# A ReLU² attention with a gated convolution FFN: products that read the two halves of their moving tile in turn

## The chip, the cores and the metric

The kernel runs on one core of a Trainium2 chip. The metric is device time in microseconds (us). PE is TensorE (products), DVE is VectorE, ACT is ScalarE, POOL is GpSimd, SP is SyncE, which issues most of the DMAs here.

## What is computed

Two stages on a batch of 4 sequences with 3136 positions, all in fp32. The first is an attention with squared ReLU in place of softmax, gated by `u`; the second a feed-forward layer whose gate is a convolution over three neighbouring positions.

```python
def _attn_ref(u, v, z):          # u, v: 4 x 3136 x 256; z: 4 x 3136 x 64
    scale = 1.0 / S
    scores = scale * np.matmul(z, z.transpose(0, 2, 1))
    attn = np.maximum(scores, 0.0) ** 2
    out = np.matmul(attn, v)
    return (u * out).astype(np.float32)

def _moe_ref(x, w_in, conv_w, w_out):   # 256 -> 1024 -> 256
    h = np.maximum(x @ w_in, 0.0)
    ...
    for k in range(K):
        conv_out += conv_w[k][None, None, :] * hp[:, k:k + S, :]
    gate = 1.0 / (1.0 + np.exp(-conv_out))
    return (h * gate @ w_out).astype(np.float32)
```

## The kernel before

Positions lie along the free axis. A batch has 6 blocks of 512 positions (`NB`) and a rest of 64; a block meets 25 tiles of 128 keys (`NJ`), so there are 24 x 25 = 600 slots. A slot takes one tile of keys through the attention for one block, and the feed-forward work of the block before is dealt out over the same slots.

To keep fp32 accuracy with `float32r` products, each operand is split into a high part and a low part (what the high part left over), and a product is made of two or three: high times high, low times high, high times low. Per slot:

- `scores`: two products of 512 columns (`zh`, then `zl`, against the block's queries `zq`) into PSUM. Since the scores are symmetric, many tiles are not computed but fetched: what was computed earlier is cut into halfwords by POOL (`part`), written to DRAM by SP (`spill`) and read back transposed (`fetch`). Such a tile stands in `tp`.
- `relu` and `square`: ACT brings the scores to SBUF with a ReLU (`t<-s`), DVE multiplies scores and ReLU in place in PSUM (`s<-s,t`). For a fetched tile, ACT or DVE squares `tp` into PSUM.
- `split_hi`, `split_lo`: ACT copies the square to `ah` (the high part), DVE subtracts it for `al` (the low part).
- `attend`: for each half of the 256 value columns, three products against `vv` accumulate in `av0`, `av1` over the block's 25 slots.

Per block and each of 8 groups `f` of 128 features: `ffn_in` (six products), `ffn_relu` (ACT from PSUM to SBUF), the three taps of the convolution and the gate (ACT, DVE), `ffn_hi` and `ffn_lo` (ACT, POOL), `ffn_out` (three products for each output half), and at the block's end `evac` and a store. The last 64 positions of all batches are done apart: `rem_scores`, `rem_attend` (25 products a batch whose moving tile is `vv`), and a feed-forward of 256 and 266 columns at the very end. `early` and `ring_score` make small pieces of a block's scores ahead of time. Seven products on zeros (`warm`) open the program.

Every product has its own weight load of 128 x 128. A moving tile is read in natural order, column after column, 512 columns of 4 bytes, or 256 or 266 in the small cases; `ring_score` reads two runs of 128. The product's columns come out in the same order, and ACT and DVE read PSUM contiguously.

The order on each engine is written out by hand: `ev` holds the calls of each slot in six classes, `LA`, `LT`, `LS` and the like say how many slots ahead each step stands, and the loop over `k` at the end issues them. Nothing is rescheduled afterwards. Every engine works through its instructions in that order; PSUM has two banks for scores (`s`), two for `ph`, and two each for `av` and `o`.

Of the kernel before, what the change touches and what calls it, by code (L numbers as in the profile page):

```python
# [81 lines left out]
def kernel(  # L82
# [94 lines left out]


    zst, vst, wst, wps = {}, {}, {}, {}
    LO, HI = slice(0, DQ), slice(DQ, P)  # L180
# [54 lines left out]
    def warm():  # L235
        x = mv.tile([P, NB], F32R, tag="gh", name="wx", bufs=3)
        nc.vector.memset(x.bitcast(F32), 0.0)
        o = ps.tile([P, 512], F32, tag="o0", name="wo")
        for _ in range(WARM):
            nc.tensor.matmul(o, lhsT=x[:, :P], rhs=x, start=True, stop=True)  # L240

# [108 lines left out]
    def ring_score(blk):  # L350
        j = blk % QB * CB + CB - 1
        dg[blk] = p = ps.tile([P, 512], F32, tag="ph", name="ph", bufs=2)
        w = slice(j * P, (j + 1) * P)
        nc.tensor.matmul(odd(p), lhsT=zh[:, w], rhs=odd(zq[blk]), start=True, stop=False)
        nc.tensor.matmul(odd(p), lhsT=zl[:, w], rhs=odd(zq[blk]), start=False, stop=True)

    def ring_relu(blk):
        p = dg[blk]
        dg[blk] = t = wk.tile([P, 1, 2 * NB], U16, tag="dg", name="dg", bufs=1)
        nc.scalar.activation(odd(t[:, 0].bitcast(F32)), odd(p), AF.Relu, scale=SC1)  # L360

# [12 lines left out]
    def scores(k):  # L374
# [9 lines left out]
        w, c = slice(j * P, (j + 1) * P), own_cols(k)  # L384
        r = zq[blk][:, c]
        nc.tensor.matmul(s[:, c], lhsT=zh[:, w], rhs=r, start=True, stop=False)  # L386
        nc.tensor.matmul(s[:, c], lhsT=zl[:, w], rhs=r, start=False, stop=True)  # L387
        sc[k] = s

    rl, pl, dq, dd, tp = {}, {}, {}, {}, {}  # L390

# [12 lines left out]
    def part(k):  # L404
# [45 lines left out]
    def relu(k):  # L450
        x = side(k)
        if at_slot(k)[2] or x or held(k):
            if held(k):
                rl[k] = tp[k] = hs.pop(at_slot(k)[0])
            if x and x < CB - 1:
                rl[k] = tp[k]
                c = own_cols(k)
                nc.scalar.activation(tp[k][:, c], sc[k][:, c], AF.Relu, scale=SC1)
            else:
# [5 lines left out]
            else:  # L465
                nc.scalar.activation(sc[k][:, :NB], tp[k], AF.Square, scale=SC1**-0.5)
            return
        rl[k] = wk.tile([P, NB], F32, tag="t", name="t", bufs=3)
        nc.scalar.activation(rl[k], sc[k][:, :NB], AF.Relu, scale=SC1)  # L469
# [15 lines left out]
    def split_hi(k):  # L485
# [17 lines left out]
    def attend(k, dcs=None):  # L503
# [5 lines left out]
        for dc in dcs or (reversed(range(DC)) if first or k == NJ - 1 else range(DC)):  # L509
# [13 lines left out]
    def early(blk):  # L523
        hs[blk] = p = ps.tile([P, 512], F32, tag="ph", name="ph", bufs=2)
        nc.tensor.matmul(p, lhsT=zp, rhs=zq[blk], start=True, stop=True)  # L525

    def early_copy(blk):
        p = hs[blk]
        hs[blk] = c = wk.tile([P, NB], F32, tag="st", name="sc", bufs=4)
        nc.scalar.copy(c, p)  # L530

# [72 lines left out]
    def rem_evac():  # L604
        rr.pop("a")
        rr["t"] = t = wk.tile([P, NB], F32, tag="t", name="re", bufs=3)
        nc.scalar.copy(t, rr.pop("o"))

# [33 lines left out]
    def gate_x(blk, eng):  # L642
        gate_half(blk, 0)
        t, o = ut[blk], pav.pop(blk)
        x = wk.tile([P, NB], F32, tag="t", name="x1", bufs=3)
        nc.scalar.mul(x, o[1], SCALE)
# [31 lines left out]
    def ffn_in(blk, f, tag="ph"):  # L678
# [3 lines left out]
        for dc in range(DC):  # L682
            nc.tensor.matmul(o, lhsT=wih[:, dc, w], rhs=xh[blk][:, dc], start=(dc == 0), stop=False)  # L683
            nc.tensor.matmul(o, lhsT=wil[:, dc, w], rhs=xh[blk][:, dc], start=False, stop=False)  # L684
        for dc in range(DC):
            nc.tensor.matmul(o, lhsT=wih[:, dc, w], rhs=xl[blk][:, dc], start=False, stop=(dc == DC - 1))  # L686
        ph[blk, f] = p
# [17 lines left out]
    def ffn_relu(blk, f):  # L705
        t, p = hb[blk, f], ph[blk, f]
        if blk == "r":
            nc.scalar.activation(seam(t)[:, :, 2 : 2 + RQ], seam(p[:, : B * RQ]), AF.Relu)
            return
        nc.scalar.activation(t[:, 2 : NB + 2], p, AF.Relu)  # L710

# [39 lines left out]
    def ffn_out(blk, f, dc, tag="o"):  # L751
# [3 lines left out]
        h, l = gg[blk, f]  # L755
        nc.tensor.matmul(o, lhsT=wol[:, f, d], rhs=h, start=(f == 0), stop=False)  # L756
        nc.tensor.matmul(o, lhsT=woh[:, f, d], rhs=h, start=False, stop=False)  # L757
        nc.tensor.matmul(o, lhsT=woh[:, f, d], rhs=l, start=False, stop=(f == FC - 1))  # L758
        if dc == DC - 1:
# [10 lines left out]
    def evac(blk, dcs=range(DC), engs=(nc.scalar, nc.scalar)):  # L770
# [7 lines left out]
        for dc in dcs:  # L778
            copy(engs[dc], ob[blk][:, dc, :e], po[blk][dc][:, :e])

# [356 lines left out]
```

## Time and profile before

| | |
|---|---|
| median of 3 runs | 1530.1 us (1529.99 to 1530.73) |
| span of the profiled execution | 1528.4 us |
| PE busy | 1518.8 us, 99%, 6781 products |
| ACT busy | 1210.8 us, 79% |
| DVE busy | 1114.9 us, 73% |
| POOL busy | 859.7 us, 56% |
| DMA queue of SP | 56.0% of 16 engines' span |

The span runs from the first to the last instruction of one profiled execution; the times are of whole runs without a profile, 1.7 us above it in the median. Engines work at once, so shares don't add up. A product is shown on PE with its full length, 0.39 us for 512 columns, but the next one starts before it ends: what a product costs in a row of products is the distance between starts. PEld is the weight load, which runs beside the products. In rows of instructions, `av<-ah,vv` gives the tile written and the tiles read, and `128x512` partitions and elements.

### The profile page before, as it was taken

Reading aid. Unit: us, or ns where it says so; the run is one execution under the profiler, and the core shown is the slowest. Engines: PE = TensorE matmul, PEld = TensorE weight load, DVE = VectorE, ACT = ScalarE, POOL = GpSimd, SP = SyncE. Lnnn points to the kernel's source line nnn. Section 1 sums busy time; section 2 is a strip of 40 time slices with the busy share of each in tenths; the row PEclk is TensorE's granted clock in tenths of the full one; section 3 lists DMA queues with packets and bytes.
Section 4 is the critical chain, followed back from the end, with each engine's and each line's share of the span. In section 5 each row is a group of like instructions: output and inputs, shape, how many; then the busy total and the mean of one; then the engine's idle time right before and its main releaser. Section 6 shows DMA issues by size and latency. Waiting matters only on the chain.

```text
span 1528.4 us, 22846 instructions
## 1 busy us (share of the span) xinstructions
PE 1518.8 (99%) x6781; PEld 1255.5 (82%) x6781; DVE 1114.9 (73%) x1714; ACT 1210.8 (79%) x2308; POOL 859.7 (56%) x1174
## 2 busy tenths in 40 slices
PE   9999999999999999999999999999999999999998
PEld 7778888888888888888888888888888888888887
DVE  8987767777777666767777766776777676677767
ACT  8888787788777878877878777877787777877767
POOL 7775555557755554555866554555586654545434
PEclk9999999999999999999999999999999999999999
DMA  6543576774545467678344565666644546466631
GB/s 201 163 141 96 150 156 144 154 164 126 157 119 140 125 138 159 141 146 183 116 143 120 143 149 125 151 154 132 155 148 134 128 122 150 120 150 151 128 67 35
DMA packets 435902, 211.03 MB, mean 138 GB/s; under 512 B 331456, under 2 KB 412608, under 8 KB 435776
## 3 DMA queue, kind: packets, MB, share of 16 engines
q1 hardware_dynamic: 435104, 209.17, 56.0%
q8 instruction: 53, 0.87, 0.2%
q14 instruction: 73, 0.60, 0.1%
q10 hardware_dynamic: 672, 0.40, 0.1%
HBM read 36.59 MB, written 86.90 MB: 81 GB/s over the span
## 4 chain that ended last, share of the span: by engine, by line
PE 96%; ACT 2%; DVE 1%; issue 1%; DMA 0%; POOL 0%; SPq 0%; ACTq 0%; POOLq 0%
PE av L514 51%; PE o L756 6%; PE o L757 6%; PE o L758 6%; PE ph L683 6%; PE ph L684 6%; PE ph L686 6%; PE s L386 4%; PE s L387 4%; PE av L596 1%; ACT t L469 0%; DVE ph L725 0%; PE ph L525 0%; DMA st<-in_z_dram 0%; ACT ah L492 0%
## 5 line engine op out<-in xcount | busy, mean ns | idle before, releaser
L514 PE MATMUL av<-ah,vv 128*128 128x512 f32 x2400 | 735.0, 390 | 1.9 <-ACT ah L492 1.6
L173 DVE TENSOR_TENSOR al<-s,ah 128x512 fp32r<-128x512 f32 x576 | 396.9, 689 | 312.0 <-PE av L514 165.8
L514 PEld LDWEIGHTS av<-ah,vv 128*128 128x128 f32 x2400 | 446.9, 188 | 93.4 <-ACT ah L492 2.0
L514 PE MATMUL av<-al,vv 128*128 128x512 f32 x1152 | 448.4, 389 | 0.1
L173 POOL TENSOR_TENSOR gl<-hb,gh 128x512 fp32r<-128x512 f32 x192 | 253.1, 1318 | 158.7 <-ACT gh L176 158.4
L725 DVE SCALAR_TENSOR_TENSOR ph<-hb,cw,ph 128x512 f32<-128x512 f32 x384 | 286.8, 747 | 5.0 <-ACT ph L720 4.4
L416 POOL COPY pl<-t 128x1024 uint16<-128x1024 uint16 (+1 forms) x257 | 261.9, 1021 | 1.8 <-DMA dq<-pl 1.6
L514 PEld LDWEIGHTS av<-al,vv 128*128 128x128 f32 x1152 | 216.3, 188 | 45.8 <-DVE al L173 0.6
L483 DVE TENSOR_TENSOR s<-s,t 128x512 f32<-128x512 f32 x275 | 191.9, 698 | 71.7 <-ACT t L469 69.9
L469 ACT ACTIVATE t<-s 128x512 f32<-128x512 f32 x277 | 165.9, 599 | 75.1 <-PE s L387 66.8
L492 ACT CAST ah<-s 128x512 fp32r<-128x512 f32 x277 | 163.5, 590 | 57.6 <-DVE s L483 57.2
L715 POOL COPY halo<-hb 128x2 f32<-128x2 f32 x160 | 31.1, 195 | 279.6 <-ACT hb L710 279.4
L732 ACT ACTIVATE ph<-ph 128x512 f32<-128x512 f32 (+1 forms) x200 | 115.6, 578 | 87.3 <-DVE ph L725 84.1
L488 ACT ACTIVATE ah<-tp 128x512 fp32r<-128x512 f32 x278 | 174.1, 629 | 3.0 <-PE av L514 2.7
L683 PE MATMUL ph<-xh,wih 128*128 128x512 f32 x384 | 149.9, 390 | 0.6 <-DVE hb L739 0.6
L756 PE MATMUL o<-gh,wol 128*128 128x512 f32 x384 | 149.8, 390 | 0.0
L684 PE MATMUL ph<-xh,wil 128*128 128x512 f32 x384 | 149.8, 390 | 0.0
L757 PE MATMUL o<-gh,woh 128*128 128x512 f32 x384 | 149.4, 389 | 0.0
L758 PE MATMUL o<-gl,woh 128*128 128x512 f32 x384 | 149.4, 389 | 0.0
L710 ACT ACTIVATE hb<-ph 128x512 f32<-128x512 f32 x192 | 114.6, 597 | 29.1 <-PE ph L686 27.6
L739 DVE TENSOR_TENSOR hb<-ph,hb 128x512 f32<-128x512 f32 x192 | 131.7, 686 | 5.5 <-ACT ph L732 0.7
L720 ACT ACTIVATE ph<-hb,cw 128x512 f32<-128x512 f32 x192 | 133.5, 695 | 0.3
(138 smaller groups left out, 2084.3 us busy)
## 6 DMA issues: line engine op xcount, KB each, us to landing
dq<-pl SPq DMA_DIRECT2D x232, 256.0 KB, 2.7
st<-in_v_dram SPq DMA_DIRECT2D x48, 256.0 KB, 3.1
ut<-in_u_dram SPq DMA_DIRECT2D x24, 512.0 KB, 4.0
out_dram<-ob SPq DMA_DIRECT2D x19, 512.0 KB, 3.8
st<-in_z_dram SPq DMA_DIRECT2D x24, 256.0 KB, 3.2
sh<-sc SPq DMA_DIRECT2D x44, 128.0 KB, 2.4
dd<-pl SPq DMA_DIRECT2D x69, 64.0 KB, 2.0
dd<-pl SPq DMA_DIRECT2D x23, 192.0 KB, 2.5
```

Of the source, the lines that this page charges most:

```text
L173: eng.tensor_tensor(out=out, in0=a, in1=b.bitcast(F32), op=ALU.subtract)
L416: nc.gpsimd.tensor_copy(pl[k], src.bitcast(U16).rearrange("p (n h) -> p h n", h=2))
L469: nc.scalar.activation(rl[k], sc[k][:, :NB], AF.Relu, scale=SC1)
L483: nc.vector.tensor_tensor(out=s, in0=s, in1=rl[k], op=ALU.mult)
L488: nc.scalar.activation(ah[k], tp.pop(k), AF.Square, scale=SC1**-0.5)
L514: nc.tensor.matmul(o, lhsT=w[:, j, d], rhs=r, start=first and i == 0, stop=last and i == len(ops) - 1)
L683: nc.tensor.matmul(o, lhsT=wih[:, dc, w], rhs=xh[blk][:, dc], start=(dc == 0), stop=False)
L684: nc.tensor.matmul(o, lhsT=wil[:, dc, w], rhs=xh[blk][:, dc], start=False, stop=False)
L725: nc.vector.scalar_tensor_tensor(out=c, in0=hb[blk, f][:, k : e + k], scalar=cw[:, f, k : k + 1], in1=c, op0=ALU.mult, op1=ALU.add,)
L756: nc.tensor.matmul(o, lhsT=wol[:, f, d], rhs=h, start=(f == 0), stop=False)
L757: nc.tensor.matmul(o, lhsT=woh[:, f, d], rhs=h, start=False, stop=False)
L758: nc.tensor.matmul(o, lhsT=woh[:, f, d], rhs=l, start=False, stop=(f == FC - 1))
```

## The change

Every moving tile is now read through `pairs`: column 0, then the first column of the second half, column 1, the second of the second half, and so on. For 512 columns the two are 1 KB apart in a partition; for 256 columns 512 bytes, for 266 columns 532. In `rem_attend` the halves are the high and low part of `vv`. The 64-column products are left as they are. Weights, accumulation, the number of products and their order stay.

The columns in PSUM then stand as 0, 256, 1, 257. They are put right where they leave PSUM: `unpair` reads every second word, first the even ones, then the odd ones, and the result lands in SBUF in natural order, through `halves`, which gives the natural order the same shape. Where a score tile is brought to SBUF by `relu` and multiplied in place by `square`, both stay shuffled (the slots in `mixed`), and `split_hi`, `split_lo` and `part` put the order right. Squares of fetched tiles are in natural order and are read so. The ring's small scores now lie compactly in 256 columns of their bank.

```diff
+    def pairs(t):
+        return t.rearrange("p (a i) -> p i a", a=2)
+
+    def halves(t):
+        return t.rearrange("p (a i) -> p a i", a=2)
+
+    def unpair(t):
+        return t.rearrange("p (i a) -> p a i", a=2)
...
-            nc.tensor.matmul(o, lhsT=x[:, :P], rhs=x, start=True, stop=True)
+            nc.tensor.matmul(o, lhsT=x[:, :P], rhs=pairs(x), start=True, stop=True)
...
-        r = zq[blk][:, c]
+        r = pairs(zq[blk][:, c])
         nc.tensor.matmul(s[:, c], lhsT=zh[:, w], rhs=r, start=True, stop=False)
         nc.tensor.matmul(s[:, c], lhsT=zl[:, w], rhs=r, start=False, stop=True)
...
-        nc.gpsimd.tensor_copy(pl[k], src.bitcast(U16).rearrange("p (n h) -> p h n", h=2))
+        src = src.bitcast(U16)
+        if k in mixed:
+            w = src.rearrange("p (i a h) -> p h a i", a=2, h=2)
+            if x == 0:
+                w = rl[k].bitcast(U16).rearrange("p (i a h) -> p h a i", a=2, h=2)
+                nc.gpsimd.tensor_copy(pl[k][:, :, :P], w[:, :, 0, P:])
+                nc.gpsimd.tensor_copy(pl[k][:, :, P:], w[:, :, 1])
+            else:
+                nc.gpsimd.tensor_copy(pl[k].rearrange("p h (a i) -> p h a i", a=2), w)
+        else:
+            nc.gpsimd.tensor_copy(pl[k], src.rearrange("p (n h) -> p h n", h=2))
...
-            nc.scalar.copy(ah[k], sc[k][:, :NB])
+            nc.scalar.copy(halves(ah[k]), unpair(sc[k][:, :NB]))

     def split_lo(k):
-        s, h = sc.pop(k)[:, :NB], ah[k]
+        s, h = (unpair if k in mixed else halves)(sc.pop(k)[:, :NB]), halves(ah[k])
...
-            sub(nc.vector, al[k], s, h)
+            sub(nc.vector, halves(al[k]), s, h)
...
-                    o, lhsT=w[:, j, d], rhs=r, start=first and i == 0, stop=last and i == len(ops) - 1
+                    o, lhsT=w[:, j, d], rhs=pairs(r), start=first and i == 0, stop=last and i == len(ops) - 1
...
-                rhs=vv[:, j].rearrange("p h d -> p (h d)"),
+                rhs=vv[:, j].rearrange("p h d -> p d h"),
...
-            out=t[:, dc], in0=o[dc], scalar=SCALE, in1=t[:, dc], op0=ALU.mult, op1=ALU.mult
+            out=halves(t[:, dc]), in0=unpair(o[dc]), scalar=SCALE, in1=halves(t[:, dc]),
+            op0=ALU.mult, op1=ALU.mult,
...
-        nc.scalar.activation(t[:, 2 : NB + 2], p, AF.Relu)
+        nc.scalar.activation(halves(t[:, 2 : NB + 2]), unpair(p), AF.Relu)
...
-            copy(engs[dc], ob[blk][:, dc, :e], po[blk][dc][:, :e])
+            copy(engs[dc], halves(ob[blk][:, dc, :e]), unpair(po[blk][dc][:, :e]))
```

The other products (`ring_score`, `early`, `ffn_in`, `ffn_out`) and the other first reads of PSUM (`ring_relu`, `early_copy`, `rem_evac`, `gate_x`, the second ReLU of `relu`) are changed in the same way.

Instructions stay in their order on every engine. What is added are 23 copies on POOL, where `part` cuts a block's first diagonal tile. Before, POOL in the first batch, with `pl<-t` the cut of a score tile, `ut` and `xl` the gated output and its low part:

```order
L416 COPY pl<-t 128x1024
L365 COPY pl<-dg 128x2x128
L173 TENSOR_TENSOR wol<-wr,woh 128x256
L416 COPY pl<-t 128x2x384
L647 TENSOR_TENSOR ut<-x_760,ut 128x512
L173 TENSOR_TENSOR xl<-ut,xh 128x512
```

After, in the same place:

```order
L434 COPY pl<-t 128x1024
L375 COPY pl<-dg 128x2x128
L173 TENSOR_TENSOR wol<-wr,woh 128x256
L431 COPY pl<-t 128x2x128
L432 COPY pl<-t 128x2x256
L668 TENSOR_TENSOR ut<-x_761,ut 128x512
L173 TENSOR_TENSOR xl<-ut,xh 128x512
```

The cut of 384 columns has become one of 128 and one of 256; line numbers moved because lines were added above.

## Rows read from the trace of the kernel before

**Rows 1.** The page: span, part 1 (busy time) and the clock row of part 2.

```profile
span 1528.4 us, 22846 instructions
...
PE 1518.8 (99%) x6781; PEld 1255.5 (82%) x6781; DVE 1114.9 (73%) x1714; ACT 1210.8 (79%) x2308; POOL 859.7 (56%) x1174
...
PEclk9999999999999999999999999999999999999999
```

**Rows 2.** The page, part 4: the chain that ended last, by engine.

```profile
PE 96%; ACT 2%; DVE 1%; issue 1%; DMA 0%; POOL 0%; SPq 0%; ACTq 0%; POOLq 0%
```

**Rows 3.** Waits of PE: who waited for whom, us in total, times, longest.

```profile
PE av L514 <- ACT ah L492: 1.6, 1, 1.6
```

**Rows 4.** The chain in order of time: start us, length us, what, how many.

```profile
184.73 2.72 PE av L514 x12
...
1056.28 2.95 PE av L514 x13
```

**Rows 5.** Timeline of PE, first 7 us: start us, length us, engine, line, operation.

```profile
2.04 1.05 PE L240 MATMUL wo<-wx 128*128 128x512 f32 x2
...
3.32 1.05 PE L240 MATMUL wo<-wx 128*128 128x512 f32 x2
...
3.75 1.05 PE L240 MATMUL wo<-wx 128*128 128x512 f32 x2
...
5.48 0.40 PE L386 MATMUL s<-zq,zh 128*128 128x512 f32 x1
5.71 0.40 PE L387 MATMUL s<-zq,zl 128*128 128x512 f32 x1
...
6.65 0.39 PE L387 MATMUL s<-zq,zl 128*128 128x512 f32 x1
```

**Rows 6.** Timeline of PE at the 256-column products, columns as in rows 5.

```profile
1489.40 0.28 PE L683 MATMUL ph<-xr,wih 128*128 128x256 f32 x1
...
1490.37 0.40 PE L686 MATMUL ph<-xr,wih 128*128 128x256 f32 x2
1490.61 0.40 PE L756 MATMUL o<-gh,wol 128*128 128x512 f32 x1
```

**Rows 7.** Four stretches: us, then busy us (instructions) of PE, PEld, DVE, ACT, POOL, clock, DMA.

```profile
0.00:38.00 38.00, 34.73 (x143) 27.41 (x144) 31.46 (x64) 33.05 (x69) 29.68 (x34) 1.00 0.66 202
38.00:115.00 77.00, 75.61 (x332) 60.92 (x331) 69.98 (x127) 67.19 (x142) 59.02 (x82) 1.00 0.52 152
115.00:1490.00 1375.00, 1374.92 (x6125) 1138.65 (x6124) 983.56 (x1469) 1080.56 (x2032) 755.64 (x1024) 1.00 0.58 138
1490.00:1529.00 39.00, 33.51 (x187) 28.56 (x185) 29.90 (x58) 29.97 (x67) 15.31 (x36) 0.98 0.11 35
```

**Rows 8.** Groups by line and shape: out<-in, shapes, xcount, busy us, mean ns.

```profile
L173 DVE TENSOR_TENSOR al<-s,ah 128x512 fp32r<-128x512 f32 x576 | 396.9, 689 | 312.0 <-PE av L514 165.8 <-ACT ah L488 87.7 <-ACT ah L492 21.1
...
L416 POOL COPY pl<-t 128x1024 uint16<-128x1024 uint16 x234 | 242.9, 1040 | 0.9 <-DMA dq<-pl 0.8
...
L492 ACT CAST ah<-s 128x512 fp32r<-128x512 f32 x277 | 163.5, 590 | 57.6 <-DVE s L483 57.2
...
L710 ACT ACTIVATE hb<-ph 128x512 f32<-128x512 f32 x192 | 114.6, 597 | 29.1 <-PE ph L686 27.6
...
L416 POOL COPY pl<-t 128x768 uint16<-128x768 uint16 x23 | 19.0, 825 | 0.8 <-DMA dq<-pl 0.8
...
L458 ACT ACTIVATE tp<-s 128x256 f32<-128x256 f32 x46 | 17.9, 389 | 7.8 <-PE s L387 7.8
...
L300 DVE TENSOR_SCALAR wp<-wr 128x256 uint32<-128x256 uint32 x8 | 3.4, 428 | 0.3
...
L173 DVE TENSOR_TENSOR al<-ph,ah 128x266 fp32r<-128x266 f32 x8 | 3.3, 427 | 0.1
...
L306 ACT ACTIVATE wr<-wr 128x256 f32<-128x256 uint32 x8 | 3.3, 406 | 0.0
...
L315 ACT ACTIVATE wr<-wr 128x256 f32<-128x256 uint32 x2 | 0.9, 434 | 0.0
```

More of the change, by code (lines that the diff above doesn't have):

```diff
@@ L353, in ring_score @@
         w = slice(j * P, (j + 1) * P)
-        nc.tensor.matmul(odd(p), lhsT=zh[:, w], rhs=odd(zq[blk]), start=True, stop=False)
-        nc.tensor.matmul(odd(p), lhsT=zl[:, w], rhs=odd(zq[blk]), start=False, stop=True)
+        o, r = p[:, : NB // 2], odd(zq[blk]).rearrange("p a n -> p n a")
+        nc.tensor.matmul(o, lhsT=zh[:, w], rhs=r, start=True, stop=False)
+        nc.tensor.matmul(o, lhsT=zl[:, w], rhs=r, start=False, stop=True)
     def ring_relu(blk):
@@ L359, in ring_relu @@
         dg[blk] = t = wk.tile([P, 1, 2 * NB], U16, tag="dg", name="dg", bufs=1)
-        nc.scalar.activation(odd(t[:, 0].bitcast(F32)), odd(p), AF.Relu, scale=SC1)
+        nc.scalar.activation(odd(t[:, 0].bitcast(F32)), unpair(p[:, : NB // 2]), AF.Relu, scale=SC1)
     def ring_part(blk):
@@ L388, in scores @@
         sc[k] = s
-    rl, pl, dq, dd, tp = {}, {}, {}, {}, {}
+    rl, pl, dq, dd, tp, mixed = {}, {}, {}, {}, {}, set()
     def rows_of(b, r):
@@ L457, in relu @@
                 c = own_cols(k)
-                nc.scalar.activation(tp[k][:, c], sc[k][:, c], AF.Relu, scale=SC1)
+                nc.scalar.activation(halves(tp[k][:, c]), unpair(sc[k][:, c]), AF.Relu, scale=SC1)
             else:
@@ L467, in relu @@
             return
+        mixed.add(k)
         rl[k] = wk.tile([P, NB], F32, tag="t", name="t", bufs=3)
@@ L524, in early @@
         hs[blk] = p = ps.tile([P, 512], F32, tag="ph", name="ph", bufs=2)
-        nc.tensor.matmul(p, lhsT=zp, rhs=zq[blk], start=True, stop=True)
+        nc.tensor.matmul(p, lhsT=zp, rhs=pairs(zq[blk]), start=True, stop=True)
     def early_copy(blk):
@@ L529, in early_copy @@
         hs[blk] = c = wk.tile([P, NB], F32, tag="st", name="sc", bufs=4)
-        nc.scalar.copy(c, p)
+        nc.scalar.copy(halves(c), unpair(p))
     def early_swap(blk):
@@ L606, in rem_evac @@
         rr["t"] = t = wk.tile([P, NB], F32, tag="t", name="re", bufs=3)
-        nc.scalar.copy(t, rr.pop("o"))
+        nc.scalar.copy(halves(t), unpair(rr.pop("o")))
     def rem_part():
@@ L645, in gate_x @@
         x = wk.tile([P, NB], F32, tag="t", name="x1", bufs=3)
-        nc.scalar.mul(x, o[1], SCALE)
+        nc.scalar.mul(halves(x), unpair(o[1]), SCALE)
         eng.tensor_tensor(out=t[:, 1], in0=x, in1=t[:, 1], op=ALU.mult)
@@ L682, in ffn_in @@
         for dc in range(DC):
-            nc.tensor.matmul(o, lhsT=wih[:, dc, w], rhs=xh[blk][:, dc], start=(dc == 0), stop=False)
-            nc.tensor.matmul(o, lhsT=wil[:, dc, w], rhs=xh[blk][:, dc], start=False, stop=False)
+            nc.tensor.matmul(o, lhsT=wih[:, dc, w], rhs=pairs(xh[blk][:, dc]), start=(dc == 0), stop=False)
+            nc.tensor.matmul(o, lhsT=wil[:, dc, w], rhs=pairs(xh[blk][:, dc]), start=False, stop=False)
         for dc in range(DC):
-            nc.tensor.matmul(o, lhsT=wih[:, dc, w], rhs=xl[blk][:, dc], start=False, stop=(dc == DC - 1))
+            nc.tensor.matmul(o, lhsT=wih[:, dc, w], rhs=pairs(xl[blk][:, dc]), start=False, stop=(dc == DC - 1))
         ph[blk, f] = p
@@ L707, in ffn_relu @@
         if blk == "r":
-            nc.scalar.activation(seam(t)[:, :, 2 : 2 + RQ], seam(p[:, : B * RQ]), AF.Relu)
+            o = seam(t)[:, :, 2 : 2 + RQ].rearrange("p (a b) n -> p a b n", a=2)
+            i = p[:, : B * RQ].rearrange("p (b i a) -> p a b i", a=2, i=RQ)
+            nc.scalar.activation(o, i, AF.Relu)
             return
-        nc.scalar.activation(t[:, 2 : NB + 2], p, AF.Relu)
+        nc.scalar.activation(halves(t[:, 2 : NB + 2]), unpair(p), AF.Relu)
     def ffn_keep(blk, f):
@@ L755, in ffn_out @@
         h, l = gg[blk, f]
-        nc.tensor.matmul(o, lhsT=wol[:, f, d], rhs=h, start=(f == 0), stop=False)
-        nc.tensor.matmul(o, lhsT=woh[:, f, d], rhs=h, start=False, stop=False)
-        nc.tensor.matmul(o, lhsT=woh[:, f, d], rhs=l, start=False, stop=(f == FC - 1))
+        nc.tensor.matmul(o, lhsT=wol[:, f, d], rhs=pairs(h), start=(f == 0), stop=False)
+        nc.tensor.matmul(o, lhsT=woh[:, f, d], rhs=pairs(h), start=False, stop=False)
+        nc.tensor.matmul(o, lhsT=woh[:, f, d], rhs=pairs(l), start=False, stop=(f == FC - 1))
         if dc == DC - 1:
```

## The prediction

> **What bounds the kernel now.** I read the page's busy shares first, then the chain, PE's waits, and last the starts of single products on the timeline. PE is busy 99% of a span of 1528.4 us, ACT 79%, DVE 73%, POOL 56% [rows 1]; the chain that ended last is PE for 96% [rows 2]; and the longest entry in PE's list of waits is one wait of 1.6 us [rows 3]. From 115 to 1490 us PE is idle for 0.08 us of 1375 [rows 7]. So the end is set by how many products there are times the distance from one start to the next, and nothing else matters while that holds. The reader should look at that distance, not at the 0.39 us printed as a product's length, since products overlap.
>
> Twelve products of 512 columns take 2.72 us and thirteen take 2.95 [rows 4]: 226.7 and 226.9 ns each. At one column per cycle of the upper of TensorE's two levels, 2.4 GHz, 512 columns need 213.3 ns. Each product is 13.4 ns, or 32 cycles, too long. Three things in the rows say what kind of excess this is.
>
> First, it belongs to the product and not to the column. Between the starts at 1489.40 and 1490.61 us lie ten products of 256 columns [rows 6], 121 ns each against 106.7 for the columns: 14 ns too long, the same as at 512. What comes once for each product is its weight load. Second, it is not there when columns arrive half as fast. After the engine had stood idle, the warm-up products start at 2.04, 3.32 and 3.75 us [rows 5]; four distances make 1.71 us, 427.5 ns each, which is 512 columns at the lower level of 1.2 GHz with nothing over. (The clock row prints full speed there; I read the level from the distance.) These products have weight loads as well. Third, its size is not fixed: from 5.48 to 6.65 us five products take 1.17 us [rows 5], 234 ns each, an excess of 21 ns. An excess that comes with the weight load, vanishes at half speed and depends on how the two stand to each other in time looks like two streams of SBUF reads that get in each other's way: the moving tile's columns and the next product's weights.
>
> **The change part by part.**
>
> *Moving reads.* Each product keeps its columns, weights and place; only the sequence of moving reads changes: column 0, column 256, column 1, column 257. A moving read now walks the tile in two halves at half the pace. At full speed the old walk covers 2048 bytes of a partition in 213.3 ns, 9.6 bytes per ns; each half is now walked at 4.8. The weight load reads 512 bytes, and in rows 6 a load fits into each 121 ns, so it walks at 4.2 or more. My estimate from these is that the two walks, which used to overtake each other, now go at about one pace, and need not meet. The trace has no product that reads in this way, so the price is bounded from both sides by its nearest rows: 213.3 ns if the excess goes, 427.5 if alternating columns costs what the lower level costs. I take 213.3, because the excess behaves like a meeting of two walks (three points above) and the change alters just that; this is an inference.
>
> The saving: 6781 products [rows 1], less 7 of the warm-up at the lower level and 8 of 64 columns (two in each of four batches, left as they are), make 6766. 6766 x 13.4 ns = 90.7 us. By stretches of rows 7: 6.3 us in the first 115 (468 products), 82.0 in the middle (6117), 2.5 in the last 39 (187).
>
> *What is late next.* In the middle 1375 us become 1293. ACT's 1080.6 us [rows 7] are then 84%, DVE's 983.6 76%, POOL's 755.6 58%. From 38 to 115 us ACT is already at 87% and DVE at 91%, and PE stands 1.39 of 77 us, 1.8% [rows 7]. At that rate the middle would lose 23 us; at best none. I take 8, a third, since DVE has much more room there. In the first 115 us the other engines are near full, so I give back half of 6.3: 3 us. In the last 39 PE waits at 33.5 of 39 for chains of other engines: half of 2.5, 1.2 us.
>
> *Stepped PSUM reads.* Columns come out as 0, 256, 1, 257, so whoever first brings a product to SBUF reads every second word of its bank, twice. On ACT that is the high copy at L492 (277), the relu of the feed-forward stage at L710 (192) and some 170 more: 565 of 512 columns and 77 of 256. On DVE it is the low part of the same 277 tiles at L173 and 25 gates. No row of before reads PSUM with a step. The nearest read every second word of SBUF: ACT takes 434 ns at L315 against 406 contiguous at L306, 28 ns on 256 columns; DVE takes 428 ns for 256 at L300 against 427 contiguous for 266 columns at L173 [rows 8], nothing. By these ACT gains 565 x 56 + 77 x 28 ns = 34 us and goes to 86% of the middle, which lies in the 8 us above. The upper bound is a column that costs double: (590 - 389) / 256 = 0.79 ns a column on ACT [rows 8], so 402 ns on 512, 243 us in all. I take the low end, the stepped rows being the nearer kind. Below nothing is excluded: no column or instruction is saved there. The DVE square and the relu before it at L469 work on the shuffled tile as it stands.
>
> *POOL.* The 234 copies at L416 of 1040 ns each [rows 8] now pick words 8 bytes apart in place of 4, and 23 copies of 768 halfwords become two. The fixed part of one is 825 - 768 x (1040 - 825)/256 = 180 ns, so 23 x 0.18 = 4 us. It is hidden while POOL is at 58%; behind each lie the spill on SP's queue and, ten slots later, the transposing fetch, which have that time. If the wider step doubled the copies, POOL would gain 262 us and stand at about 1120, still under ACT.
>
> **The sum.** 1528.4 - 90.7 + 8 + 3 + 1.2 = 1449.9. The median of the runs is 1.7 us above the span of the profiled execution, so 1451.6.
>
> **The rivals.**
>
> *The reads have nothing to do with it.* The 32 cycles may be what a change of weights costs at the upper level, whatever the moving pattern. For it: the excess comes once per product and is the same for all tiles and addresses. Against: it is absent at the lower level, and varies from 13.4 to 21 ns. Then PE stays at 1518.8, ACT and DVE have their present room, and the time is 1530, within 3 us. The Trainium skill, "TensorE: Matmul & The Clock Gate", in the step-by-step part of Part 2, gives PE two independent SBUF read ports, so that loading weights takes nothing from a running product. By that rule 90.7 us stay and the time is 1530; the trace's lower level without excess speaks against it.
>
> *Alternating costs more than it saves.* Every column now lies elsewhere than the one before, 1 KB apart, and PE could be fed only at the pace of the lower level. Place: every product. Point from which it decides: 226.7 ns a product; 13.4 ns on 512 columns is all there is to win, so a single extra cycle in sixteen columns cancels it. Price at the far end: 427.5/226.7 = 1.886, PE 1518.8 x 1.886 = 2864, with the 9.6 us it is idle and 1.7 a time of 2876. At the near end, the worse of the two excesses on record, 234 ns: 6766 x 7.3 = 49 us, 1580. For it: full speed asks for a column each 0.42 ns and the rows show a stream already held up. Against: nothing in the trace; no product reads so. The Trainium skill, "SBUF — State Buffer", under "Specifications (TRN2)", says that SBUF lines are 16 bytes and that full bandwidth wants two hits or more in a line. Natural order makes four fp32 hits in a row, the changed order one at a time, so by that rule it would be this rival; no row of before shows such a read.
>
> *Stepped PSUM reads are dear.* At double price ACT has 1211 + 243 = 1454 us of work, DVE 1115 + about 165 = 1280. ACT then sets the pace; at 95% of the span that is 1531, with 1.7 a time of 1532, and half the surcharge gives about 1470. The gain on PE would be there and be eaten.
>
> **How the numbers follow.** Forecast 0.60, all of it faster; its own range is 1439 (all excess gone, nothing late: 1437.7 + 1.7) to 1512 (half the excess stays, 45 us, and 23 us of waits in the middle). Reads without effect 0.15, all within 0.2% (3 us, about what a measurement of this kernel can tell from no change). Alternating dear 0.15, all slower. PSUM dear 0.10: 0.04 faster, 0.02 the same, 0.04 slower. Faster 0.64, same 0.17, slower 0.19. The range goes from 1439 to 1550, over the second and most of the last case, and leaves out the dear alternation.
>
> **What the profile after would show.** If I am right: twelve products of L514's successor in 2.56 to 2.6 us, ten of 256 columns in 1.07 to 1.1, the same busy ns at DVE's low part, 590 to 650 at ACT's high copy, and the first entries of a few us each in PE's waits, on ACT or DVE. If the reads have no effect: 226.7 again. If alternating is dear: distances above 227, PE at 99% still, and all other engines with more room. If PSUM is dear: 13 ns less a product, ACT's copies near 1000 ns, and PE waiting for ACT. I would be wrong above all if the excess is the weights' own.

## The result, and the profile after

The changed kernel takes 1513.0 us in the median of 4 runs (1510.2 to 1515.1), against 1530.2 for the kernel before beside it: a ratio of 0.9886, with a 95% interval from 0.9872 to 0.9900. It is 1.1% faster. The direction was forecast; the size was not: 17 us came instead of 78.

The page of the changed kernel: span, busy time (share of the span), the clock row and the chain by engine. Beside [rows 1] and [rows 2]:

```profile
span 1512.5 us, 22772 instructions
...
PE 1467.8 (97%) x6781; PEld 1266.5 (84%) x6781; DVE 1139.8 (75%) x1714; ACT 1205.4 (80%) x2308; POOL 977.0 (65%) x1197
...
PEclk9999999999899999999999999999999999999999
...
PE 64%; ACT 11%; DVE 8%; POOL 7%; issue 5%; DMA 3%; SPq 1%; ACTq 0%; POOLq 0%; DVEq 0%
```

PE has 51 us less to do, as hoped for in kind, but its idle time grew from 9.6 to 44.7 us, the chain is PE's for 64% in place of 96%, and POOL, which should have gained 4 us, gained 117. The clock row has a dip that [rows 1] did not have.

The chain in order of time (start, length, what, count), beside [rows 4]:

```profile
191.73 2.59 PE av L535 x12
...
398.90 7.41 DVE s L482
...
767.80 7.32 DVE s L482
```

Twelve products take 2.59 us, 215.8 ns each, where it was 2.72 (226.7). So 10.9 ns went of the 13.4. Two entries are new, each a single DVE instruction of more than 7 us. The groups (line, engine, operation, shapes, count, then busy us and mean ns of one, then idle time before them and its causes), beside [rows 8]:

```profile
L173 DVE TENSOR_TENSOR al<-s,ah 128x512 fp32r<-128x512 f32 x576 | 396.8, 689 | 263.6 <-PE av L535 125.6 <-ACT ah L509 100.9 <-ACT ah L513 22.0
L434 POOL COPY pl<-t 128x1024 uint16<-128x1024 uint16 x234 | 359.4, 1539 | 1.5 <-DMA dq<-pl 1.3
...
L513 ACT CAST ah<-s 128x512 fp32r<-128x512 f32 x277 | 163.1, 589 | 83.8 <-DVE s L504 83.4
L734 ACT ACTIVATE hb<-ph 128x512 f32<-128x512 f32 x192 | 114.4, 596 | 17.6 <-PE ph L708 15.4
```

The stepped reads of PSUM on ACT and DVE last what the contiguous ones did (590, 597 and 689 ns in [rows 8]). The stepped cut on POOL went from 1040 to 1539 ns: 234 of them are the 117 us.

Where PE's time went shows in its waits (who waited for whom, us in total, times, longest; [rows 3] had 1.6 us as its largest entry):

```profile
PE s L396 <- DVE ah L173: 21.7, 7, 6.7
PE s L396 <- DVE al L173: 8.0, 11, 3.2
```

And here is one of the three long waits on the timeline, first POOL, then DVE and PE (start, length, engine, line, operation, tiles, idle time before it and what ended it):

```profile
397.76 1.44 POOL L173 TENSOR_TENSOR vv<-st,vv 128x512 fp32r<-128x512 f32 x1
398.98 0.35 POOL L739 COPY ends<-hb 128x2 f32<-128x2 f32 x1
399.10 1.74 POOL L434 COPY pl<-t 128x1024 uint16<-128x1024 uint16 x1
400.57 0.61 POOL L436 COPY pl<-tp 128x256 uint16<-128x256 uint16 x1
400.93 1.47 POOL L173 TENSOR_TENSOR gl<-hb,gh 128x512 fp32r<-128x512 f32 x1
402.13 1.25 POOL L436 COPY pl<-sh 128x1024 uint16<-128x1024 uint16 x1
403.13 1.47 POOL L173 TENSOR_TENSOR vv<-st,vv 128x512 fp32r<-128x512 f32 x1
404.34 0.40 POOL L724 COPY hb<-halo 128x2 f32<-128x2 f32 x1
404.46 1.29 POOL L434 COPY pl<-t 128x1024 uint16<-128x1024 uint16 x1
```

```profile
398.29 0.69 DVE L173 TENSOR_TENSOR al<-s,ah 128x512 fp32r<-128x512 f32 x1 [1.68 <-ACT ah L509]
398.90 7.41 DVE L482 SCALAR_TENSOR_TENSOR s<-sh 128x512 f32<-128x512 f32 x1
```

```profile
400.67 0.38 PE L535 MATMUL av<-al,vv 128*128 128x512 f32 x1
407.75 0.80 PE L396 MATMUL s<-zq,zh 128*128 128x512 f32 x1 [6.70 <-DVE ah L173]
408.34 0.63 PE L397 MATMUL s<-zq,zl 128*128 128x512 f32 x1
408.76 0.63 PE L780 MATMUL o<-gh,wol 128*128 128x512 f32 x1
...
413.46 0.39 PE L705 MATMUL ph<-xh,wih 128*128 128x512 f32 x1
```

DVE squares a tile that was computed ahead (`sh`, both operands in SBUF). Such a square takes 0.69 us when nothing is in its way. Here POOL works through eight more instructions without a gap, until 405.75, and the square ends 0.56 us after that. The other two, from 767.78 and 1136.78 us, stand at the same instructions a batch later each, and end 0.56 us after POOL's row too. PE's next scores wait for a split that stands behind the square on DVE. So PE stands for 6.7 us, and when it starts again its products are 0.42 to 0.43 us apart until 413.46 (the first distance is 0.59), twice the 0.216 of before: it comes back at the lower of its two levels, 1.2 GHz. The windows of the stretch, and of one near 97 us (us, then busy us and instructions of PE, PEld, DVE, ACT, POOL, then the granted clock, the DMA share and GB/s), say so too:

```profile
407.75:413.46 5.71, 5.71 (x14) 4.54 (x15) 4.00 (x6) 2.26 (x4) 0.00 (x0) 0.50 0.32 92
413.46:420.00 6.54, 6.54 (x32) 5.74 (x31) 3.69 (x6) 4.90 (x9) 4.38 (x5) 1.00 0.20 50
...
96.98:102.68 5.70, 5.70 (x13) 4.53 (x14) 4.66 (x10) 2.26 (x4) 1.83 (x3) 0.50 0.36 110
```

A stall costs PE 7.08 - 0.22 = 6.9 us between starts, and the thirteen distances at the lower level 5.71 - 13 x 0.216 = 2.9 more. Three of them make 29 us.

In the kernel before the same square lasted 0.69 us. POOL stood idle for 1.5 us ahead of the copy of `ends`, and the square came in only as the cut behind that copy ended (timeline of before, POOL and DVE):

```profile
398.91 0.19 POOL L715 COPY ends<-hb 128x2 f32<-128x2 f32 x1 [1.50 <-ACT hb L710]
400.00 0.69 DVE L462 SCALAR_TENSOR_TENSOR s<-sh 128x512 f32<-128x512 f32 x1
```

In the changed kernel that pause is gone, and the square comes in 0.2 to 0.3 us before the end of the sum that stands ahead of the copy, at all three places.

A fourth, smaller stall gives the 3.2 us in the list of PE's waits. Its DVE instruction reads one SBUF operand and writes SBUF, and it lasts as long as POOL's next three instructions, until 95.97:

```profile
92.84 3.28 DVE L305 TENSOR_SCALAR wr<-wr 128x256 uint32<-128x256 uint32 x1
```

PE comes back at the lower level here too (the last of the windows above). By the same working this stall costs 3.56 - 0.22 = 3.3 us between starts and 5.70 - 13 x 0.216 = 2.9 more, 6 us in all.

### The profile page after: what moved, and what is told of

The parts are those of the page before. It is cut to its first block, busy times and chain, and to the rows that moved or that the text cites. A ratio compares the mean times of both kernels' runs of the same rounds, so it can differ in the third digit from the quotient of the medians.

```text
span 1512.5 us, 22772 instructions
## 1 busy us (share of the span) xinstructions
PE 1467.8 (97%) x6781; PEld 1266.5 (84%) x6781; DVE 1139.8 (75%) x1714; ACT 1205.4 (80%) x2308; POOL 977.0 (65%) x1197
## 4 chain that ended last, share of the span: by engine, by line
PE 64%; ACT 11%; DVE 8%; POOL 7%; issue 5%; DMA 3%; SPq 1%; ACTq 0%; POOLq 0%; DVEq 0%
PE av L535 33%; PE ph L705 4%; PE o L782 4%; PE o L780 4%; PE o L781 4%; PE ph L706 4%; PE ph L708 4%; PE s L396 3%; DVE s L482 3%; PE s L397 3%; POOL pl L434 3%; DVE ph L749 2%; PE av L617 1%; DMA dq<-pl 1%; ACT ph L744 1%
## 5 line engine op out<-in xcount | busy, mean ns | idle before, releaser
L535 PE MATMUL av<-ah,vv 128*128 128x512 f32 x2400 | 712.4, 381 | 1.7 <-ACT x L667 1.3
L535 PEld LDWEIGHTS av<-ah,vv 128*128 128x128 f32 x2400 | 451.8, 190 | 65.9 <-ACT x L667 1.7
L535 PE MATMUL av<-al,vv 128*128 128x512 f32 x1152 | 439.9, 382 | 0.7
L434 POOL COPY pl<-t 128x1024 uint16<-128x1024 uint16 x234 | 359.4, 1539 | 1.5 <-DMA dq<-pl 1.3
L396 PE MATMUL s<-zq,zh 128*128 128x512 f32 x323 | 123.7, 383 | 30.0 <-DVE ah L173 21.7
L705 PE MATMUL ph<-xh,wih 128*128 128x512 f32 x384 | 146.1, 380 | 1.1 <-DVE hb L763 1.1
L706 PE MATMUL ph<-xh,wil 128*128 128x512 f32 x384 | 145.5, 379 | 0.0
```

What stands on the lines that cost most here:

```text
L434: nc.gpsimd.tensor_copy(pl[k].rearrange("p h (a i) -> p h a i", a=2), w)
L535: nc.tensor.matmul(o, lhsT=w[:, j, d], rhs=pairs(r), start=first and i == 0, stop=last and i == len(ops) - 1)
L705: nc.tensor.matmul(o, lhsT=wih[:, dc, w], rhs=pairs(xh[blk][:, dc]), start=(dc == 0), stop=False)
L706: nc.tensor.matmul(o, lhsT=wil[:, dc, w], rhs=pairs(xh[blk][:, dc]), start=False, stop=False)
```

## The experiments

### What the order of reading costs: PE alone

Nothing of the kernel is computed; PE makes stretches of 30 products in a row on one tile, each stretch reading it in another order.

```diff
+    for i in range(30):
+        nc.tensor.matmul(o[i % 2], lhsT=ws[i % 2], rhs=x[:, 0:512], start=True, stop=True)
+    for i in range(30):
+        nc.tensor.matmul(o[i % 2], lhsT=ws[i % 2], rhs=in_turn(h, 2), start=True, stop=True)
...
```

> Nothing of the computation is left but stretches of 30 products that differ in how they read their operands; PE alone works. Theory (two walks that meet): the excess over 213.3 ns depends on how the pace of the moving walk stands to that of the weight walk. Natural 226.7 ns, two halves in turn 215.7 as in the changed kernel; four or eight parts in turn (a half or a quarter of that pace) above 215.7; weights with a step of two words against natural columns about 216 (both walks fast), and against halves in turn about 227. Rival A (any alternation between distant columns frees the weight load): two, four and eight parts all 215.7, the weights' step changes nothing. Rival B (a jump each column costs, and the gain is a matter of bytes per line): runs of 2 and 4 columns in turn are faster than runs of 1. Rival C (the excess is the weights' own): 64 weight columns halve the excess, and weights that don't change keep it.

Timeline of PE (start, length, then as above). The distance from one stretch's start to the next, by 30, is what a product costs. In order: natural, halves, quarters and eighths in turn, evens then odds, runs of two and of four columns from the two halves in turn, then halves 16 bytes further apart; below, natural order with weights of every second word, and the next stretch:

```profile
18.44 6.96 PE L118 MATMUL o<-x,w 128*128 128x512 f32 x30
25.24 6.64 PE L120 MATMUL o<-x,w 128*128 128x512 f32 x30
31.72 8.65 PE L122 MATMUL o<-x,w 128*128 128x512 f32 x30
40.20 14.86 PE L124 MATMUL o<-x,w 128*128 128x512 f32 x30
54.88 13.71 PE L126 MATMUL o<-x,w 128*128 128x512 f32 x30
68.42 10.02 PE L128 MATMUL o<-x,w 128*128 128x512 f32 x30
78.27 7.67 PE L130 MATMUL o<-x,w 128*128 128x512 f32 x30
85.77 6.64 PE L132 MATMUL o<-x,w 128*128 128x512 f32 x30
...
98.72 7.16 PE L136 MATMUL o<-x 128*128 128x512 f32 x30
105.72 6.64 PE L138 MATMUL o<-x 128*128 128x512 f32 x30
```

Natural order costs 226.7 ns, two halves in turn 215.8, quarters 283, eighths 487 to 489, evens then odds 451, runs of two 328, runs of four 250. So the gain belongs to the order of moving reads, and only two pieces, a column of each at a time, have it. My picture of two walks at equal pace fell here: weights in steps of two words, which walk twice as far, should have changed the halves and helped natural order, and gave 215.8 and 233. With 64 weight columns natural order still took 230, with one unchanging weight tile 227. Weights in steps of four words load in 310 to 332 ns, and then both orders take 235 to 237.

The Trainium skill, "SBUF — State Buffer", under "Specifications (TRN2)", asks for two hits or more in a 16-byte line. The probe disagrees on both sides: halves in turn hit a line once at a time and are the fastest, evens then odds hit each line twice in a row and take twice as long.

### How far apart the two pieces lie

```diff
+    def near(n):
+        return h.rearrange("p (b a i) -> p b i a", a=2, i=n)
```

> PE alone, stretches of 30 products of 512 columns, distance between starts. Natural order 226.7 and halves in turn 215.8 as in the first probe. New: two runs of columns in turn that lie 4, 8, 16, 32, 64 or 128 columns apart (16 to 512 bytes), and halves 516, 768, 1024 and 1536 columns apart; natural order beginning 4 and 8 bytes later; halves beginning 16 and 128 bytes later. Theory (two 16-byte pieces can be held open at once, so any two runs in turn will do): 215.8 at every distance from 4 columns up. Rival (the two must lie far apart, by where in SBUF they stand): 226 to 235 for the near ones, 215.8 from some distance on. Rival B (it hangs on the start address, as natural order does with 227 to 232): halves that begin later give 220 and more.

The chain in order of time: natural order, halves, runs 16 bytes apart (four columns), and natural order beginning 4 bytes later:

```profile
18.90 6.80 PE o L124 x30
25.70 6.47 PE o L126 x30
32.18 6.47 PE o L128 x30
...
96.93 7.11 PE o L148 x30
```

Every distance from 16 bytes to 6 KB gives 6.47 or 6.48 us for 30, 215.8 ns. Natural order varies with where the tile begins: 237 ns when it begins 4 bytes later, 234 at 8, and 232 at 16 and 128 bytes; two pieces in turn give 215.8 at 16 and 128 bytes as well. The theory of two pieces that can be held open at once fits these distances, but not the runs of two and of four columns, which keep to two pieces and are slower; what in the read path makes the difference was not shown.

### The two sides of the change apart

First, `pairs` alone: PE reads in halves, and the reads of PSUM and POOL's cut stay contiguous (the columns land in another order). Second, all the rest alone: PE reads in natural order, and PSUM and the cut are read in steps (here, too, columns land in another order).

```diff
     def unpair(t):
-        return t.rearrange("p (i a) -> p a i", a=2)
+        return t.rearrange("p (a i) -> p a i", a=2)
...
-        mixed.add(k)
```

> The moving reads of the change alone: PSUM is read contiguously and POOL cuts words 4 bytes apart as before, so columns stand in a shuffled order (the sums are of the wrong columns). Theory (POOL's dearer cut is what eats the gain): POOL's cut back at 1.04 us, the square of the held tile never above 1 us, PE's waits near those of before; 1455 to 1470 us. Rival (a PE that is 5% faster outruns ACT and DVE in any case): 1490 to 1513.

```diff
     def pairs(t):
-        return t.rearrange("p (a i) -> p i a", a=2)
+        return t
```

> The change without its moving reads: columns are read in natural order, all else is as in the changed kernel, stepped PSUM reads and dearer cuts included (the sums are of the wrong columns). Theory (POOL's cut is hidden as long as PE is slow): 226.7 ns a product and 1530 to 1536 us. Rival (the cut costs by itself, through DVE that stands behind POOL): 1545 to 1580.

The reads alone: 1475.3 us, a ratio of 0.9640 [0.9626, 0.9654], which is 55 us gained, and 5 us more time than the upper end of what I expected. The rest alone: 1532.0, 1.0013 [1.0003, 1.0022], 2 us lost; POOL's cut there:

```profile
L434 POOL COPY pl<-t 128x1024 uint16<-128x1024 uint16 x234 | 259.2, 1110 | 1.0 <-DMA dq<-pl 0.4 <-POOL ends L739 0.2 <-ACT ah L513 0.2
```

The cut takes 1110 ns with the 8-byte step, and 1539 only where PE reads in halves. By themselves the two sides would make 1477; together they make 1513. About 36 us belong to their meeting.

### The cut back in order

The change with another place for the repair: the ReLU reads PSUM in steps and writes SBUF in natural order, DVE multiplies in place through stepped PSUM, and POOL cuts in 4-byte steps as before.

```diff
-        nc.scalar.activation(rl[k], sc[k][:, :NB], AF.Relu, scale=SC1)
+        nc.scalar.activation(halves(rl[k]), unpair(sc[k][:, :NB]), AF.Relu, scale=SC1)
...
-            s = sc[k][:, :NB]
-            nc.vector.tensor_tensor(out=s, in0=s, in1=rl[k], op=ALU.mult)
+            s = unpair(sc[k][:, :NB])
+            nc.vector.tensor_tensor(out=s, in0=s, in1=halves(rl[k]), op=ALU.mult)
```

> The change with the order put right one step earlier: the ReLU at the score tile reads PSUM with a step and writes SBUF in natural order, DVE squares in place through stepped PSUM reads and writes, and POOL cuts words 4 bytes apart, in one copy. Theory (POOL's cut at 8 bytes is the cause): cut 1.04 us, ACT 0.60 and DVE 0.70 us unchanged, 1455 to 1475 us. Rival (stepped PSUM accesses of DVE or the faster PE are the cause): 1495 to 1520.

It takes 1475.6 us, 0.9646 [0.9630, 0.9663], just above the upper end of what I expected: better than both kernels, by 54.4 us on the one before. Its page and groups:

```profile
PE 1453.2 (99%) x6781; PEld 1261.3 (86%) x6781; DVE 1110.6 (75%) x1714; ACT 1203.8 (82%) x2308; POOL 851.6 (58%) x1174
...
L426 POOL COPY pl<-t 128x1024 uint16<-128x1024 uint16 x234 | 242.6, 1039 | 0.5 <-ACT ah L503 0.3
```

The cut is back at 1039 ns, PE's longest wait is 1.5 us and the clock row has no dip. Moving the repair from POOL to engines that read PSUM is worth 37.4 us.

### The held tile squared on ACT

The changed kernel with the square of `sh` on ACT and the cut as slow as it is; then the same on the version just shown.

```diff
-        return k // NJ % QB >= DS and k % 2 == 1 or held(k)
+        return k // NJ % QB >= DS and k % 2 == 1
```

> The changed kernel with one edit: the square of the held tile (one in each block from the third on, 22 in all) is made by ACT instead of DVE; POOL keeps its dearer cut. Theory (three of these squares stand 6.7 to 7.4 us behind a train of POOL instructions, PE stands still for 6.8 us each time and its clock drops after it): the three stalls and the drops behind them go, about 3 x (6.8 + 3.4) = 31 us, so 1480 to 1490 us; the drop near 96 us, which comes from another DVE instruction, stays. Rival (the stalls move to the next DVE instruction that reads SBUF alone): 1500 to 1513.

> The order put right at the ReLU (POOL's cut as before) and the held tile squared by ACT. Theory (with the short cut there is no stall of that kind left): 1470 to 1478, no different from the short cut alone. Rival (waits behind POOL still cost some us at the held tile): below 1468.

1483.7 us, 0.9696 [0.9682, 0.9711], and 1477.3, 0.9657 [0.9641, 0.9673]. In the first the cut still takes 1546 ns, but the long waits of PE and the dip in its clock row are gone (one stretch of 3.4 us at the lower level is left, from 61.0 us):

```profile
PE s L396 <- DVE al L173: 5.2, 11, 1.3
```

So of the 37.4 us, 29.3 went through DVE's squares, which is the 29 counted on the timeline. The slow cut costs the other 6 to 8 in smaller waits (1483.7 against 1477.3 with the square on ACT in both). The fourth stall, which I expected to stay, is gone here as well: the longest wait is 1.3 us. Other waits of the first 120 us stand in its place, so what it is worth by itself is known from its own rows alone.

### Who slows the cut

POOL alone with the kernel's cuts; then POOL, DVE and ACT each reading SBUF in steps and contiguously, while PE is idle, reads in natural order, and reads in halves (in this one PE's streams and the other engines' stretches were out of step, so some stretches are mixed).

> Nothing of the computation is left: POOL makes ten copies of 1024 halfwords of each kind, words 4 bytes apart, the same in four dimensions, 8 bytes apart in four dimensions, 8 bytes apart in three, and half as many at 8 bytes; then trains of 3, 8 and 8 copies (the last with the 8-byte step) while DVE multiplies an SBUF tile by itself. Theory (the step, not the number of dimensions, sets POOL's price, and a DVE instruction with two SBUF operands waits until a train of POOL instructions ends): 1.04, 1.04, 1.55, 1.55, 0.85 us; the DVE product lasts about as long as what is left of the train, 2, 7 and 11 us. Rival A (the fourth dimension is what costs): 1.04, 1.55, 1.55, 1.04. Rival B (DVE gets in after the POOL instruction under way): never above 2.3 us.

> Nothing of the computation is left: POOL copies 1024 halfwords with words 4 bytes apart, then 8, then 4 again, while PE stands still, streams 110 products in natural order, and streams 110 with two halves in turn; then DVE and ACT copy 512 words contiguously and every second word in the same three settings. Theory (POOL's 8-byte walk through SBUF is slowed by PE's two walks, as the cut takes 1.55 us in the changed kernel, 1.11 where the moving reads are natural, and 1.07 in the stretches where PE stands still): 1.04 in all three settings at 4 bytes; 1.08, 1.10 and 1.55 at 8 bytes. DVE and ACT with every second word: longer by 15 to 25% beside two halves in turn, as L309 (512 against 428 ns), no change at the contiguous ones. Rival (ACT or DVE beside it, not PE, is what slows the cut): 1.08 in all three.

Alone a cut in 4-byte steps takes 1040 ns and one in 8-byte steps 1084. So the step itself costs 4%, and both expectations that it costs half fell. Beside PE it depends on PE's order: in the second of these runs the cut in 8-byte steps takes 1090 ns beside natural order. ACT copying every second word of SBUF, with PE idle, in natural order, and in halves (groups, as above):

```profile
L180 ACT COPY e<-r 128x512 f32<-128x512 f32 x8 | 7.0, 875 | 0.2
L172 ACT COPY e<-r 128x512 f32<-128x512 f32 x8 | 5.3, 659 | 0.2
L164 ACT COPY e<-r 128x512 f32<-128x512 f32 x8 | 5.2, 646 | 0.2
```

646, 659 and 875 ns, from the lowest row up. DVE reading every second word goes from 426 to 521 beside halves. Contiguous copies stay where they are, 616 on ACT and 427 on DVE, and so does POOL's cut in 4-byte steps, 1039 ns in the version with the cut in order. POOL's clean pair comes from a later run, twelve equal rows of instructions of which the first six stood beside PE reading in halves: a cut in 8-byte steps with PE busy, and one with PE idle:

```profile
24.86 1.54 POOL L116 COPY c<-g 128x1024 uint16<-128x1024 uint16 x1
...
112.74 1.07 POOL L116 COPY c<-g 128x1024 uint16<-128x1024 uint16 x1
```

1.54 us is what the changed kernel shows. The Trainium skill, "SBUF — State Buffer", under "Who interferes with whom", lets only the port pair shared by DVE and GpSimd cause contention. Here ACT and POOL are slowed by nothing but the order in which PE reads.

### Why DVE was shut out for 7.4 us

Four probes of POOL's rows of instructions, with a DVE square of one SBUF tile that comes in during them. In the first the square came in while POOL's first copy had not got going (that copy took 2.4 us), and it tells nothing of a row under way. In the second and third POOL and DVE are alone; in the fourth PE reads in halves beside the first six of twelve rows.

```diff
+        for i in range(8):
+            nc.gpsimd.tensor_copy(c[i], g.bitcast(U16).rearrange("p (n h) -> p h n", h=2))
+        for j in range(4):
+            nc.vector.memset(w, 0.0)
+        nc.vector.scalar_tensor_tensor(out=q, in0=m, scalar=2.0, in1=m, op0=ALU.mult, op1=ALU.mult)
```

> Nothing of the computation is left: DVE multiplies an SBUF tile by itself while POOL is in the middle of a train of eight copies into eight tiles (none waits for another), then of eight copies into one tile (each waits for the one before), then of three into three tiles. Theory (the DVE instruction gets in only where POOL leaves a gap): about 5 to 7 us in the first train, until its end; below 2 us in the second; about 2 us in the third. Rival (it gets in after the instruction under way, and the 7 us in the kernel have another cause): below 2 us in all three.

> POOL and DVE alone, four trains on POOL of eight cutting copies (128x1024 halfwords, about 1.04 us each, 8 us a train). While a train runs DVE fills a PSUM bank four times, which touches no SBUF, and then squares a tile of 512 columns into PSUM. In the first and fourth train the copies write eight different tiles and follow without a gap, and both operands of the square lie in SBUF; the second is the same with one operand in PSUM; in the third the copies write the same tile one after the other, with a small gap between, and both operands lie in SBUF. Theory (two operands from SBUF wait until POOL's gapless train lets go): the square lasts 4 to 6 us in the first and fourth train, 0.6 to 0.7 in the second, at most 1.7 in the third. Rival A (it waits for one POOL instruction at most, and the 7.4 us of the changed kernel have another cause): 0.6 to 1.7 us in all four. Rival B (any DVE read of SBUF waits for the train): 4 to 6 us in the second too.

> POOL and DVE alone, eight trains on POOL. Trains 0 to 2: six sums of 512 columns with both operands in SBUF (1.25 us each in the changed kernel). Trains 3 to 7: the row that stands on POOL during the 7.4 us (sum, copy of 64, cut, cut, sum, cut, sum, copy of 64, cut, sum), in trains 6 and 7 with cuts in steps of 8 bytes. DVE comes in during the first instruction, in train 4 during the second or third: a square with both operands in SBUF (trains 0, 3, 4, 6), one with an operand in PSUM (1, 5, 7), a scaling of one SBUF tile into another (2). Copies alone have not locked DVE out: there POOL waited 0.9 us for DVE. Theory (once POOL holds the way to SBUF through a sum of two SBUF operands, it keeps it for what follows without a gap): square and scaling last 5 us and more in trains 0, 2, 3, 6, to the train's end, and 0.65 in 1, 5, 7; in train 4 either. Rival (POOL's queue has no part in it; the 7.4 us come from something that only the full kernel has, such as PE's or the DMAs' traffic): 0.6 to 1.7 us in all eight.

> Twelve times the mixed row of POOL instructions with cuts in steps of 8 bytes, and a DVE square with both operands in SBUF that comes in after one to six fills of a PSUM bank, so at another place of the row each time (0.7 to 4 us after its start). Beside the first six rows PE reads a tile in two halves without a pause; beside the last six it is idle. Theory A (PE's reading in halves slows POOL and so changes who gets the way to SBUF): at least one square of the first six waits over more than one end of a POOL instruction, 2 us and more, and none of the last six. Theory B (what locks DVE out depends on the place in the row at which it comes in): long waits at the same places in both halves. Theory C (neither; it takes something else of the full kernel): in all twelve the square begins at the next end of a POOL instruction and lasts 2.3 us at most.

In none of them did the square wait for the row. Nor did it in the run with POOL's cuts alone, where I expected waits of 2, 7 and 11 us and the longest square took 1.52. In the second and third it lasted 0.64 us, and POOL paid: one copy took 1.99 us in place of 1.04, a sum 1.87 to 1.94 in place of 1.04; with one operand in PSUM POOL paid nothing. (In most rows of the third probe the square came in with the row's first instruction, which is the weaker test.) In the fourth the longest wait, beside PE's reading in halves, was this:

```profile
32.67 1.57 DVE L149 SCALAR_TENSOR_TENSOR q<-m 128x512 f32<-128x512 f32 x1
```

It got in when the cut that was running ended, and so did the longest with PE idle, 1.10 us. The full kernels do the same nearly always. Of their DVE instructions that last 0.15 us and more beyond the shortest of their kind, some 30 in the kernel before and some 35 in the changed one wait over one end of a POOL instruction, and a handful over two. The changed kernel alone has longer ones, the one near 93 us and these three. So the meeting of a DVE instruction that works on SBUF with POOL is shown. Why it lost eight times in a row at these places, and not elsewhere, is not. Neither a gapless row, nor sums in it, nor PE's halves beside it are enough by what was tried. No probe had the square come in 0.2 to 0.3 us before the end of a sum, as all three do; that alone is not enough either, since a DVE instruction of the changed kernel at 87.08 us, of one SBUF operand, came in so and got in as the sum ended (it lasted 0.47 us).

## Why the prediction was right or wrong

**The bound.** Right: PE's distance between starts set the time, and it moved. *Reads without effect* and *alternating dear* fell with 215.8 ns. The second was near: four pieces in place of two would have cost 283.

**The saving.** Mis-sized. The step took all 13.4 ns, down to 213.3; 10.9 went. 6766 x 10.9 = 74 us in place of 90.7. The rows of before had no distance of 512 columns under 226.7 at the upper level, so 213.3 was an end of the range, and I took the end. The Trainium skill, "TensorE: Matmul & The Clock Gate", under "Wait — 56ns, not 53.3ns?", gives 215.7 ns for 512 columns at the upper level. The trace now agrees, to 0.1 ns, for two halves in turn, though not for natural order; an estimate with that figure, 6766 x 11.0 = 74, would have been right.

**Why the excess goes.** The three rows spoke for reads that get in each other's way, and the order of the moving reads does decide. That the weight load is the other party, and equal pace the cure, was inferred and not borne out.

**Late next.** Near. The version with the cut in order has what this step was made for: its span of 1472.2 is 56.2 under the 1528.4 of before, so 74 - 56 = 18 us came back, where I had 12. PE's idle time on the page grew by 9.4 (9.6 to 19.0). Counted from start to start, what lies beyond a product's own distance grew by some 15, since the page hides short pauses behind the printed length of a product; the last 3 stay open.

**Stepped PSUM reads.** Right in kind, and cheaper than the low end that I took: they cost nothing on ACT or DVE (589, 596 and 689 ns), where I gave ACT 34 us from rows that read SBUF in steps. *PSUM dear* fell.

**POOL.** This is the step that failed. I put the wider step at nothing, without a row for it (the 4 us were for the split copies), called the cut hidden while POOL is at 58%, and asked only whether POOL's sum of busy time stays under ACT's. The doubled cut was in the text, as 262 us "still under ACT". The cut grew by half, 117 us, POOL stood at 65%, and it still cost 37 us: not by its sum, but because POOL's row came late and without gaps where a DVE instruction needed to get in, with PE behind it and the clock behind PE. Three such places cost 29 us and a fourth 6. Two things were missing. One is that the new order of PE's reads could change what other engines' reads cost, which no row of before could show. The other is that an engine off the path can hold one on it: the bound was set against POOL's total, and never against the places where POOL and DVE meet.

In one line of profiled spans: 1528.4 - 74 + 18 = 1472 is the version with the cut in order, where 1450 was forecast; 29 for three stalls and their low clock, 6 for the fourth and some 5 for smaller waits make the 1512.5.

**The range.** That 1513.0 lies inside 1439 to 1550 is luck. The upper part of the range stood for half of the excess staying and for dear PSUM reads, and neither happened.

## What to carry to other kernels

Reading the moving tile as two pieces in turn is worth 11 ns a product of 512 columns in `float32r` here, and the pieces may lie as close as 16 bytes. Put the columns right where PSUM is read, since stepped PSUM reads on ACT and DVE were free, and keep reads of SBUF in 8-byte steps off the other engines while PE reads so. An engine at 60% is not free room: look at which instructions of a busier engine must get in between its own.

## What the runs showed of the hardware that I had not expected

- PE's reading in two halves slows SBUF reads of other engines in 8-byte steps: a halfword cut on POOL takes 1.54 us in place of 1.07, every second word on ACT 875 ns in place of 646, on DVE 521 in place of 426. Contiguous reads keep their time, and so does POOL's cut in 4-byte steps.
- Natural order in `float32r` costs 226.7 to 237 ns by its start address, two pieces in turn, a column of each at a time, 215.8 at any start and distance tried (16 bytes to 6 KB).
- A DVE square of two SBUF operands waited 7.4 us over eight POOL instructions, three times in a run. In the probes either POOL waited, 0.8 to 0.95 us, or the square waited for the one copy that was running, up to 1.57 us in all.
- After 6.7 us without a product PE came back at 1.2 GHz for 5.7 us, which added 2.9 us to a stall of 6.9; the stall of 3.3 us near 93 us was followed by as much.
